# Keys and queries turned per pair of heads, and the globals' scores moved to other PSUM banks

## The chip, the cores and the metric

The kernel runs on one core of a Trainium2 chip. The metric is the device time of one launch in microseconds (us), the median of several runs. Five engines work beside each other and meet through semaphores: TensorE (PE), VectorE (DVE), ScalarE (ACT), GpSimd (POOL) and SyncE (SP), which issues most of the DMA transfers.

## The reference

Three layers follow one another: an attention with local and global tokens, a soft mixture of experts, and a mixture of experts with one expert a token. Only the first is touched.

```python
# q_l, k_l, v_l: (4, 8, 512, 64); q_g, k_g, v_g: (4, 8, 32, 64); window = 32
k_all = np.concatenate([k_g, k_l], axis=2)
s_g   = scale * np.matmul(q_g, k_all.transpose(0, 1, 3, 2))   # globals see all 544 keys
out_g = np.matmul(sm(s_g), v_all)
mask  = np.abs(pos[:, None] - pos[None, :]) <= window
s_ll  = np.where(mask, scale * np.matmul(q_l, k_l.transpose(0, 1, 3, 2)), -1e9)
s_lg  = scale * np.matmul(q_l, k_g.transpose(0, 1, 3, 2))
out_l = np.matmul(sm(np.concatenate([s_lg, s_ll], axis=-1)), np.concatenate([v_g, v_l], axis=2))
x = concat(out_g, out_l) -> (2304, 512)
x = moe(x)    # phi (512, 32), 8 experts of 4 slots, w1 and w2
out = moe2(x) # top-1 of 8 experts, capacity 576
```

## The kernel before

**Units and steps.** The attention is cut into 8 units, each one batch and half of its heads (four heads, two pairs). A unit has four Local steps (128 queries of all four heads each) and one Global step (the 32 global queries of four heads). The Global stands after the second Local; in the first unit it stands last, and in the last unit first.

**What a step issues.** The steps are staggered. In step k the program issues A of step k (scores), B of step k−1 (transposes of the probabilities), D1 of step k−3 (transposes of the result x), C of step k−2 (probabilities times values) and D2 of step k−4 (router logits lp of x). Between them stand the transposes of the next unit's keys and queries, and in some steps work of the second layer. The order on PE and POOL is the order of this code; the order on DVE, ACT and SP is chosen by the framework's scheduler.

**Scores of a Local step.** A writes 16 small matmuls into one half of each of two PSUM banks, `sc0` and `sc1`; `turn()` alternates the halves. Four DVE instructions (L335) add the mask, take the row maximum and move the scores to SBUF as P, and four exponentials on ACT (L337) follow.

**Scores of a Global step.** Its 544 keys are written in four pieces (L397): 192 and 64 columns into the half of `sc0`, 192 into the half of `sc1`, and 96 into a tile of the pool ps_x (`sg`). Five DVE instructions (L400 to L404) make the row maximum, four ACT exponentials (L406) write P.

**Keys and queries.** Keys arrive in tiles of 2 x 96 tokens (three tiles and six transfers a unit; the last transfer has 32 tokens), since the key buffer `kext` holds blocks of 96 local keys followed by 32 global ones. A tile's four transposes (both pairs of heads) fill one PSUM tile pk, which DVE empties for one pair and ACT for the other (L297). Queries arrive in two tiles of 2 x 128 tokens; each tile's four transposes (pq) are emptied the same way into one of two buffers `qtr`.

**The other names.** pt and pts: transposed probabilities of a Local step and their SBUF copy; ptg, pgg and ptsg, pgsg: those of a Global step. px and pxg: products with the values. pxt, xt: transposed x and its copy. lp, lpg: logits in PSUM; lpt, lpsg: their SBUF copies. c1 and c2 hold values rearranged for queries that straddle blocks (c2's copy on ACT is L280). The PSUM pool ps_tr has four banks, which pk, pq, pt, pxt, lp, ptg, pgg and some tiles of the second layer share.

**Transfers.** A unit's values come in eight transfers (v_g, five of 96 tokens, two of 32). All of these are issued on SP, in one queue with the 32 weight transfers of 1 MB each.

Of the kernel before, what the change touches and what calls it, by code (L numbers as in the profile page):

```python
# [37 lines left out]
def kernel(  # L38
# [119 lines left out]
    with ExitStack() as actx:  # L158
# [6 lines left out]
        qpool = actx.enter_context(tc.tile_pool(name="qpool", bufs=2))  # L165
# [20 lines left out]
        qtr = [persm.tile([128, 2, 256], F32, name=f"qtr{i}") for i in range(NQ)]  # L186
# [50 lines left out]
        def load_k(b, hf, g):  # L237

            hs = slice(4 * hf, 4 * hf + 4)
            knt[b, hf, g] = t = kpool.tile([96, 2, 4, 64], F32, tag="kn", name=f"kn{b}{hf}{g}")  # L240
            for m in range(2):
                n = 32 if m and g == 2 else 96
                o = 192 * g + 96 * m
                nc.sync.dma_start(t[0:n, m], k_l[b, hs, o:o + n].rearrange("h p d -> p h d"))

        def load_q(b, hf, j):
            hs = slice(4 * hf, 4 * hf + 4)
            t = qpool.tile([128, 2, 4, 64], F32, tag="qn", name=f"qn{b}{hf}{j}")
            for i in range(2):
                o = 256 * j + 128 * i  # L250
                nc.sync.dma_start(t[:, i], q_l[b, hs, o:o + 128].rearrange("h p d -> p h d"))
            qnt[b, hf, j] = t
# [35 lines left out]
        def unit_T(b, hf, g):  # L288
            ke, kn = kext[(2 * b + hf) % NB2], knt[b, hf, g]
            ps = ps_tr.tile([128, 2, 2, 96], F32, tag="tr", name=f"pk{b}{hf}{g}")  # L290
            for m in range(2):
                n = 32 if m and g == 2 else 96
                for pr in range(2):
                    T.transpose(ps[:, pr, m, 0:n], kn[0:n, m, 2 * pr:2 * pr + 2].rearrange("p h d -> p (h d)"), ident[0:n, 0:n])
            if g < 2:
                for pr, copy in enumerate((V.tensor_copy, S.copy)):
                    copy(ke[:, pr, 256 * g:256 * g + 256].rearrange("d (m c) -> d m c", m=2)[:, :, 0:96], ps[:, pr])  # L297
            else:
                V.tensor_copy(ke[:, :, 512:608], ps[:, :, 0])
                S.copy(ke[:, :, 640:672], ps[:, :, 1, 0:32])  # L300

        nqb = [0]
        qbs = {}

        def pair_Q(b, hf, j):
            qbs[b, hf, j] = qt = qtr[nqb[0] % NQ]
            nqb[0] += 1
            qn = qnt[b, hf, j]
            ps = ps_tr.tile([128, 2, 2, 128], F32, tag="tr", name=f"pq{b}{hf}{j}")
            for pr in range(2):  # L310
                for t in range(2):
                    T.transpose(ps[:, pr, t], qn[:, t, 2 * pr:2 * pr + 2].rearrange("p h d -> p (h d)"), ident)
            for pr, copy in enumerate((V.tensor_copy, S.copy)):
                copy(qt[:, pr].rearrange("d (t q) -> d t q", t=2), ps[:, pr])

        class Local:
# [5 lines left out]
            def A(self):  # L322
                ke, qt, u = kext[self.i], qbs[self.b, self.hf, self.u // 2], self.u
# [3 lines left out]
                for pr in range(2):  # L327
                    for c in range(4):
                        blk = 4 * u + c
                        o = 0 if blk == 0 else 544 if blk == 15 else 32 * (blk - 1 + (blk - 1) // 3)  # L330
                        for hp in range(2):
                            x = slice(64 * hp, 64 * hp + 64)
                            T.matmul(ps[hp][32 * c:32 * c + 32, pr], lhsT=qt[x, pr, 32 * (blk % 8):32 * (blk % 8) + 32], rhs=ke[x, pr, o:o + 128], start=True, stop=True, skip_group_check=True)  # L333
# [38 lines left out]
            def D2(self):  # L372
# [7 lines left out]
                V.tensor_copy(lpt[r, 128 * u:128 * u + 128], lp[r])  # L380

        class Global:
# [5 lines left out]
            def A(self):  # L388
                b, hf, ke = self.b, self.hf, kext[self.i]
                p1, p2 = turn()  # L390
                p3 = ps_x.tile([128, 96], F32, tag="x", name=f"sg{self.n}")

                lo = ke[:, :, 0:640].rearrange("p a (m c) -> p a m c", c=128)[:, :, :, 0:96]
                for ps, kk in ((p1[:, 0:192].rearrange("p (m c) -> p m c", c=96), lo[:, :, 0:2]), (p1[:, 192:256], ke[:, :, 608:672]),
                               (p2[:, 0:192].rearrange("p (m c) -> p m c", c=96), lo[:, :, 2:4]), (p3, lo[:, :, 4])):
# [3 lines left out]
                mx = work.tile([128, 5], F32, tag="mxg", name=f"mxg{self.n}")  # L399
                V.tensor_reduce(mx[:, 0:1], p1, AX.X, ALU.max)  # L400
                V.tensor_reduce(mx[:, 1:2], p2[:, 0:192], AX.X, ALU.max)
                V.tensor_reduce(mx[:, 2:3], p3, AX.X, ALU.max)
                V.tensor_reduce(mx[:, 3:4], mx[:, 0:3], AX.X, ALU.max)
                V.tensor_scalar_mul(mx[:, 4:5], mx[:, 3:4], -0.125)  # L404
                for o, ps in ((0, p1[:, 0:192]), (192, p2[:, 0:192]), (384, p3), (480, p1[:, 192:256])):
                    S.activation(P[:, o:o + ps.shape[1]], ps, AF.Exp, bias=mx[:, 4:5], scale=0.125)  # L406

            def B(self):
# [4 lines left out]
                V.tensor_copy(self.pts[0:96], pt)  # L413
# [201 lines left out]

        LQ = 2
        load_k(*units[0], 0)
        load_g(gnat_k, k_g, (0,))
        load_q(*units[0], 0)
        load_k(*units[0], 1)  # L620
        load_k(*units[0], 2)
        load_v(*units[0])
        spread_g(*units[0])
        load_q(*units[0], 1)
# [5 lines left out]
        unit_T(*units[0], 0)  # L630
# [3 lines left out]
        pair_Q(*units[0], 0)  # L634
        unit_T(*units[0], 1)
        unit_T(*units[0], 2)
# [5 lines left out]
        for k in range(ns - 1):  # L642
# [3 lines left out]
            j = (nloc + 1) // 2  # L646
            if u >= 0 and nloc % 2 and 2 * j < nl:
                pair_Q(*units[j // 2], j % 2)
# [5 lines left out]
            knext = []  # L654
            for g in range(3) if k == T0 else (u - (n < len(units) - 2),) if n and (u >= 0 and n == len(units) - 2 and u < 3 or u > 0 and n < len(units) - 2) else ():
                if n + 1 < len(units):
                    unit_T(*units[n + 1], g)
                    if g < 2:
                        unit_G(*units[n + 1], g)
                    if n + 2 < len(units):  # L660
                        knext.append(g)
# [17 lines left out]
            for g in knext:  # L679
                load_k(*units[n + 2], g)  # L680
# [19 lines left out]
            if k < ns:  # L700
                if u >= 0:
                    j = nloc // 2 + LQ
                    if nloc % 2 == 0 and 2 * j < nl:
                        load_q(*units[j // 2], j % 2)
                    if nloc == 0:
                        for g in range(3):
                            load_k(*units[1], g)
# [746 lines left out]
```

## Time and profile before

| | |
|---|---|
| median of 3 runs | 312.44 us (309.96 to 313.95) |
| profiled execution | 313.62 us, of which the span from the first to the last instruction is 311.8 us |
| mean granted TensorE clock | 0.948 |
| attention | from the start to about 175 us |
| weight stage of the second layer (ph, L883) | from 175.6 us |
| third layer | to the end |

Busy time of an engine is given in us of the span. A wait of an engine is the idle time before an instruction, with the instruction that ended it. The clock is given as a share of full speed.

### The profile page before, as it was taken

The page shows a single profiled execution, that of the slowest core. Times are in us where ns is not written, and L with a number is a line of the kernel's source. Part 1 is how long each engine was busy: PE and PEld are TensorE (multiplying, and loading weights), DVE is VectorE, ACT ScalarE, POOL GpSimd, SP SyncE. Part 2 cuts the span into 40 slices and gives each one's busy share as a digit, 9 for nine tenths or more (in the row PEclk, how much of TensorE's full clock was granted, in tenths as well). Part 3 has the DMA queues.
Part 4 walks back from the last instruction along what each step waited for, and adds up shares of the span by engine and source line. Part 5 has one row for each costly group of instructions (what it writes and reads, how often), then busy time and mean ns, then how long its engine had stood idle before and what let it go on. Part 6 is the DMA issues. An engine that isn't in the chain of part 4 may idle for free. (4 is left out here: it accounts for less than half of the span.)

```text
span 311.8 us, 10396 instructions
## 1 busy us (share of the span) xinstructions
PE 269.3 (86%) x4139; PEld 186.2 (60%) x4139; DVE 176.8 (57%) x763; ACT 136.7 (44%) x374; POOL 98.9 (32%) x191
## 2 busy tenths in 40 slices
PE   7778789879898988778689999998988699999992
PEld 5456567657676656566555644435456368877881
DVE  6364558657786866767775640016996479533100
ACT  2664537665667657754563110000452384132200
POOL 5815604640736454163223110011821001111121
PEclk9997879997999999999999999997899589999998
DMA  5766767787676897979689599999999200001010
GB/s 129 162 147 139 220 183 189 164 218 221 194 227 152 251 291 204 275 193 369 208 295 343 153 395 393 395 292 263 384 298 401 90 0 19 29 27 44 36 68 35
DMA packets 82896, 63.12 MB, mean 202 GB/s; under 512 B 57724, under 2 KB 65916, under 8 KB 82832
## 3 DMA queue, kind: packets, MB, share of 16 engines
q1 hardware_dynamic: 82144, 60.13, 63.9%
q0 software_dynamic: 688, 2.18, 1.9%
q8 instruction: 35, 0.57, 0.8%
q14 instruction: 29, 0.24, 0.2%
HBM read 55.66 MB, written 6.68 MB: 200 GB/s over the span
## 5 line engine op out<-in xcount | busy, mean ns | idle before, releaser
L337 ACT ACTIVATE P<-P,nmx 128x128 f32<-128x128 f32 x128 | 41.2, 391 | 21.5 <-DVE nmx L335 21.3
L335 DVE CUSTOM_DVE_ANT_0 P<-sc,mask 128x128 f32<-128x128 f32 x128 | 29.6, 285 | 14.7 <-PE sc L333 14.3
L333 PE MATMUL sc<-kext,qtr 64*32 64x128 f32 x1024 | 23.8, 289 | 11.4 <-ACT P L406 8.8
L271 POOL COPY c<-nat 32x520 f32<-32x520 f32 (+1 forms) x16 | 11.5, 721 | 68.0 <-PE px L355 47.0
L1222 POOL DMA_INDIRECT out_dram<-ys,idu x9 | 9.0, 998 | 71.1 <-ACT ys L1219 57.5
L346 ACT COPY pts<-pt 128x512 f32<-128x512 f32 (+1 forms) x32 | 18.1, 564 | 21.4 <-PE pt L345 21.4
L355 PE MATMUL px<-c,pts 128*32 128x65 f32 x640 | 23.1, 231 | 3.5 <-issue 3.5
L333 PEld LDWEIGHTS sc<-kext,qtr 64*32 64x32 f32 x1024 | 13.7, 110 | 19.6 <-ACT P L406 10.8
L355 PE MATMUL px<-nat,pts 128*32 128x65 f32 x384 | 22.8, 233 | 0.4 <-issue 0.4
L345 PE MATMUL pt<-ident,P 128*128 128x128 f32 x128 | 21.7, 295 | 0.0
L1183 ACT ACTIVATE hh<-phh 128x512 fp32r<-128x512 f32 x20 | 11.6, 598 | 21.2 <-PE phh L1180 15.1
L355 PEld LDWEIGHTS px<-c,pts 128*32 128x32 f32 x640 | 17.3, 114 | 6.0 <-issue 5.6
L1087 PE MATMUL pga<-oh,rec 128*128 128x128 f32 (+3 forms) x68 | 17.3, 349 | 3.8 <-DVE oh L1076 3.0
L1207 PE MATMUL py<-wh,hh 128*128 128x512 f32 (+1 forms) x72 | 20.3, 404 | 0.0
L1207 PE MATMUL py<-wl,hh 128*128 128x512 f32 (+1 forms) x72 | 20.0, 394 | 0.0
L1207 PE MATMUL py<-wh,hl 128*128 128x512 f32 (+1 forms) x72 | 19.4, 391 | 0.0
L355 PEld LDWEIGHTS px<-nat,pts 128*32 128x32 f32 x384 | 16.9, 115 | 2.6 <-issue 1.7
L1087 PEld LDWEIGHTS pga<-oh,rec 128*128 128x128 f32 x68 | 11.6, 208 | 10.2 <-DVE oh L1076 4.8
L345 PEld LDWEIGHTS pt<-ident,P 128*128 128x128 f32 x128 | 15.3, 149 | 2.8 <-issue 1.8
L1186 DVE SCALAR_TENSOR_TENSOR hl<-phh,hh 128x512 fp32r<-128x512 f32 x20 | 13.3, 688 | 5.6 <-ACT hh L1183 5.5
L883 PE MATMUL ph<-w,sT 128*32 128x256 f32 x256 | 15.9, 382 | 0.0
L1207 PEld LDWEIGHTS py<-wh,hh 128*128 128x128 f32 (+1 forms) x72 | 12.9, 186 | 4.3 <-ACT hh L1183 0.8
(307 smaller groups left out, 604.1 us busy)
## 6 DMA issues: line engine op xcount, KB each, us to landing
w<-in_moe_w_dram SPq DMA_DIRECT2D x32, 1024.0 KB, 7.4
out_dram<-zt SPq DMA_DIRECT2D x8, 544.0 KB, 10.2
qn<-in_q_l_dram SPq DMA_DIRECT2D x32, 128.0 KB, 5.4
w1b<-in_moe_w_dram SPq DMA_DIRECT2D x4, 1024.0 KB, 6.6
w2b<-in_moe_w_dram SPq DMA_DIRECT2D x8, 512.0 KB, 7.8
kn<-in_k_l_dram SPq DMA_DIRECT2D x40, 96.0 KB, 2.6
nat<-in_v_l_dram SPq DMA_DIRECT2D x40, 96.0 KB, 3.4
nat<-in_v_l_dram SPq DMA_DIRECT2D x16, 32.0 KB, 2.2
```

The costliest lines, as they stand in the source:

```text
L271: G.tensor_copy(c1[0:32, m0:m1], n[32:64, m0:m1])
L333: T.matmul(ps[hp][32 * c:32 * c + 32, pr], lhsT=qt[x, pr, 32 * (blk % 8):32 * (blk % 8) + 32], rhs=ke[x, pr, o:o + 128], start=True, stop= ...
L335: V.tensor_tensor_reduce(out=P[:, h], in0=ps[h % 2][:, h // 2], in1=mask[:, u], scale=-0.125, scalar=3.0e38, op0=ALU.add, op1=ALU.min, acc ...
L337: S.activation(P[:, h], P[:, h], AF.Exp, bias=nmx[:, h:h + 1], scale=-1.0)
L345: T.transpose(pt[:, c - h.start], self.P[:, c], ident)
L346: (V.tensor_copy if j else S.copy)(self.pts[:, h], pt)
L355: T.matmul(px[32 * c:32 * c + 32, h], lhsT=self.pts[:, h, 32 * c:32 * c + 32], rhs=vv[:, h], start=True, stop=True, skip_group_check=True)
L883: T.matmul(ph[32 * qf:32 * qf + 32], lhsT=sT[c // 2][:, c % 2], rhs=wt[:, c % 2, 256 * qf:256 * qf + 256], start=(c == 0), stop=(c == 3), ...
L1087: T.matmul(pga[0][:, 0:m], lhsT=rec[:, t], rhs=oh[0][:, q, 0:m], start=(k == 0), stop=(k == len(todo) - 1), skip_group_check=True)
L1183: S.activation(hh, ph[0], AF.Relu)
L1186: V.scalar_tensor_tensor(hl, ph[0], 0.0, hh.bitcast(F32), ALU.max, ALU.subtract)
L1207: T.matmul(py[0], lhsT=a[:, fc, o:o + nm], rhs=w[:, fc], start=(py[1] == 0), stop=(py[1] == 23))
```

## The change

Keys and queries of a unit are each loaded by four transfers of 128 tokens into one tile with four token blocks (both kinds share a pool of three buffers). Transposes go pair by pair: the four token blocks of one pair of heads fill one PSUM bank, and one engine empties it, DVE for the first pair and ACT for the second. For keys that is one copy of 480 and one of 32 columns, for queries one of 512. `qtr` holds a whole unit. Keys of the next unit are turned in the second and third Local step, queries of both pairs in the fourth.

Values come in seven transfers: v_g, one for each head (all 480 tokens of five blocks), and two of 32 tokens.

The Global's scores go into two tiles of ps_tr: `sg` with 480 columns and `sh` with 64. Four DVE instructions make the row maximum, two exponentials follow. The copy of lp to lpt (L380 before, L373 after) and the copy of ptg to ptsg (L413, L404) go from DVE to ACT.

```diff
-        qtr = [persm.tile([128, 2, 256], F32, name=f"qtr{i}") for i in range(NQ)]
+        qtr = [persm.tile([128, 2, 512], F32, name=f"qtr{i}") for i in range(NQ)]
...
+        def load_kq(to, name, src, b, hf, ts):
+            hs = slice(4 * hf, 4 * hf + 4)
+            if ts.start == 0:
+                to[b, hf] = kpool.tile([128, 4, 4, 64], F32, tag="kq", name=f"{name}{b}{hf}")
+            for t in range(ts.start, ts.stop):
+                nc.sync.dma_start(to[b, hf][:, t], src[b, hs, 128 * t:128 * t + 128].rearrange("h p d -> p h d"))
...
-            for m in range(6):
-                w = 96 if m < 5 else 32
-                nc.sync.dma_start(n[0:w, m, :, 0:64], v_l[b, hs, 96 * m:96 * m + w].rearrange("h p d -> p h d"))
+            for h in range(4):
+                nc.sync.dma_start(n[0:96, 0:5, h, 0:64], v_l[b, 4 * hf + h, 0:480].rearrange("(m p) d -> p m d", p=96))
+            nc.sync.dma_start(n[0:32, 5, :, 0:64], v_l[b, hs, 480:512].rearrange("h p d -> p h d"))
...
+        def turned(x, pr, ts, name):
+            ps = ps_tr.tile([128, ts.stop - ts.start, 128], F32, tag="tr", name=f"{name}{pr}{ts.start}")
+            for t in range(ts.start, ts.stop):
+                T.transpose(ps[:, t - ts.start], x[:, t, 2 * pr:2 * pr + 2].rearrange("p h d -> p (h d)"), ident)
+            return ps.rearrange("d t p -> d (t p)")
...
+        def unit_Q(b, hf, pr, copy, ts=slice(0, 4)):
+            copy(qtr[(2 * b + hf) % NQ][:, pr, 128 * ts.start:128 * ts.stop], turned(qnt[b, hf], pr, ts, f"pq{b}{hf}"))
...
-                V.tensor_copy(lpt[r, 128 * u:128 * u + 128], lp[r])
+                S.copy(lpt[r, 128 * u:128 * u + 128], lp[r])
...
-                p1, p2 = turn()
-                p3 = ps_x.tile([128, 96], F32, tag="x", name=f"sg{self.n}")
+                p1 = ps_tr.tile([128, 480], F32, tag="tr", name=f"sg{self.n}")
+                p2 = ps_tr.tile([128, 64], F32, tag="tr", name=f"sh{self.n}")
...
-                for o, ps in ((0, p1[:, 0:192]), (192, p2[:, 0:192]), (384, p3), (480, p1[:, 192:256])):
-                    S.activation(P[:, o:o + ps.shape[1]], ps, AF.Exp, bias=mx[:, 4:5], scale=0.125)
+                for o, ps in ((0, p1), (480, p2)):
+                    S.activation(P[:, o:o + ps.shape[1]], ps, AF.Exp, bias=mx[:, 3:4], scale=0.125)
...
-                V.tensor_copy(self.pts[0:96], pt)
+                S.copy(self.pts[0:96], pt)
...
+            if nx and u == 3:
+                unit_Q(*nx, 0, V.tensor_copy)
...
+            for pr in range(2) if k == T0 else (u - 1,) if n and 0 < u < 3 else ():
+                if nx:
+                    unit_T(*nx, pr, S.copy if pr else V.tensor_copy)
+                    unit_G(*nx, pr)
+            if nx and u == 3:
+                unit_Q(*nx, 1, S.copy)
```

**First place: PE in the Global step of the fifth unit.** Before, from the previous Global's logits (lpg) through the four score pieces (L397) to pxt; the numbers behind the names are those of single buffers, and a matmul of this type is two instructions where the row has x2:

```order
L452 MATMUL lpg_2021<-xtg_1898,phi_sb 32x32 x2
L397 MATMUL sc_172<-kext_161,qgbd 64x192 x2
L397 MATMUL sc_172<-kext_161,qgbd 64x64 x2
L397 MATMUL sc_173<-kext_161,qgbd 64x192 x2
L397 MATMUL sg_2029<-kext_161,qgbd 64x96 x2
L345 MATMUL pt_2050<-ident,P_1931 128x128 x4
L368 MATMUL pxt_2056<-ident,x_2004 128x128 x2
```

After:

```order
L443 MATMUL lpg_1930<-xtg_1816,phi_sb 32x32 x2
L389 MATMUL sg_1938<-kext_158,qgbd 64x480 x2
L389 MATMUL sh_1939<-kext_158,qgbd 64x64 x2
L338 MATMUL pt_1953<-ident,P_1851 128x128 x4
L361 MATMUL pxt_1959<-ident,x_1917 128x128 x2
```

The score pieces are two instead of four, and none of them names a bank `sc`, which the next Local step's scores use; the order around them is the same.

**Second place: ACT in the same step and the start of the next.** Before:

```order
L280 COPY c_166<-nat_162 64x520
L346 COPY pts_2049<-pt_2050 128x512
L370 COPY xt_2059<-pxt_2056 128x256
L406 ACTIVATE P_2038<-sc_172,mxg_2039 128x192
L406 ACTIVATE P_2038<-sc_173,mxg_2039 128x192
L406 ACTIVATE P_2038<-sg_2029,mxg_2039 128x96
L406 ACTIVATE P_2038<-sc_172,mxg_2039 128x64
L337 ACTIVATE P_2087<-P_2087,nmx_2088 128x128 x4
L370 COPY xt_2136<-pxt_2133 128x256
```

After:

```order
L276 COPY c_163<-nat_159 64x520 x2
L339 COPY pts_1952<-pt_1953 128x512
L363 COPY xt_1962<-pxt_1959 128x256
L397 ACTIVATE P_1944<-sg_1938,mxg_1945 128x480
L397 ACTIVATE P_1944<-sh_1939,mxg_1945 128x64
L373 COPY lpt<-lp_1986 64x128
L330 ACTIVATE P_1990<-P_1990,nmx_1991 128x128 x4
L404 COPY ptsg_2021<-ptg_2016 96x512
L302 COPY kext_160<-pk_2028 128x5x96
```

Four exponentials have become two, and the copies of lpt and ptsg stand in ACT's row, ptsg behind the four exponentials of the next Local step.

**Third place: ACT in the fourth Local step of the unit.** Before, from a key copy (kext) through the exponentials (P) and the query copy (qtr) to xt:

```order
L297 COPY kext_163<-pk_2125 128x2x96
L337 ACTIVATE P_2175<-P_2175,nmx_2176 128x128 x4
L314 COPY qtr_167<-pq_2201 128x256
L346 COPY pts_2208<-pt_2209 128x512
L300 COPY kext_163<-pk_2215 128x2x32
L370 COPY xt_2225<-pxt_2222 128x256
```

After:

```order
L363 COPY xt_2039<-pxt_2036 128x256
L373 COPY lpt<-lp_2068 64x128
L330 ACTIVATE P_2072<-P_2072,nmx_2073 128x128 x4
L339 COPY pts_2104<-pt_2105 128x512
L307 COPY qtr_165<-pq_2111 128x512
L363 COPY xt_2120<-pxt_2117 128x256
L373 COPY lpt<-lp_2173 64x128
```

The query copy has 512 columns instead of 256 and stands behind pts instead of ahead of it, and an lpt copy stands ahead of the exponentials.

## Rows read from the trace of the kernel before

**Rows 1.** The page: busy time of each engine in us, its share of the span, and the number of instructions.

```profile
PE 269.3 (86%) x4139; PEld 186.2 (60%) x4139; DVE 176.8 (57%) x763; ACT 136.7 (44%) x374; POOL 98.9 (32%) x191
```

**Rows 2.** Four of PE's waits from 25 to 160 us: engine, tile and line that waited, what ended the wait; us in total, times, longest us.

```profile
PE sc L333 <- ACT P L406: 8.8, 7, 1.8
PE pxg L427 <- issue: 4.1, 2, 2.2
PE px L355 <- issue: 2.6, 2, 2.2
PE lpg L452 <- ACT pts L346: 0.8, 3, 0.3
```

**Rows 3.** Stretches of time: length, then busy us and number of instructions of PE, PEld (PE's weight loads), DVE, ACT and POOL, then granted clock, DMA share and GB/s.

```profile
25.00:160.00 135.00, 113.19 (x2821) 84.10 (x2812) 93.37 (x495) 82.20 (x249) 60.34 (x89) 0.96 0.78 224
20.00:40.00 20.00, 15.18 (x294) 11.46 (x296) 10.65 (x49) 9.85 (x29) 9.77 (x14) 0.83 0.72 171
40.00:60.00 20.00, 18.06 (x440) 13.62 (x438) 13.97 (x76) 12.49 (x37) 6.36 (x10) 0.91 0.70 188
60.00:80.00 20.00, 16.64 (x380) 12.25 (x381) 13.81 (x72) 11.35 (x36) 8.07 (x13) 0.91 0.74 195
80.00:100.00 20.00, 16.96 (x468) 12.89 (x467) 14.01 (x76) 13.84 (x41) 11.23 (x18) 1.00 0.75 201
...
160.00:180.00 20.00, 18.44 (x302) 11.38 (x298) 12.85 (x54) 6.94 (x24) 3.78 (x25) 1.00 0.69 242
180.00:200.00 20.00, 19.54 (x248) 8.54 (x251) 3.59 (x15) 2.65 (x7) 1.86 (x9) 1.00 1.03 399
```

**Rows 4.** Timeline of PE from 95 to 102 us, a Global step of the fifth unit and the Local step behind it: start us, duration us, line and operation; in brackets the idle time before it and what ended that.

```profile
95.15 0.99 PE L397 MATMUL sc<-kext,qgbd 128*64 128x192 f32 x12
95.97 0.34 PE L397 MATMUL sg<-kext,qgbd 128*64 128x96 f32 x4
96.23 0.66 PE L345 MATMUL pt<-ident,P 128*128 128x128 f32 x4
96.72 0.38 PE L368 MATMUL pxt<-ident,x 128*128 128x128 f32 x2
...
97.54 0.39 PE L378 MATMUL lp<-xt,phi_sb 128*32 128x128 f32 x4
99.08 0.67 PE L333 MATMUL sc<-kext,qtr 64*32 64x128 f32 x32 [1.16 <-ACT P L406]
99.68 0.64 PE L411 MATMUL ptg<-ident,P 128*96 128x128 f32 x4
...
100.38 0.49 PE L294 MATMUL pk<-ident,kn 96*128 96x96 f32 x4
100.71 0.38 PE L368 MATMUL pxt<-ident,x 128*128 128x128 f32 x2
...
101.53 0.41 PE L378 MATMUL lp<-xt,phi_sb 128*32 128x128 f32 x4
101.88 0.34 PE L333 MATMUL sc<-kext,qtr 64*32 64x128 f32 x8
```

**Rows 5.** Timeline of ACT in the same place.

```profile
96.98 0.59 ACT L346 COPY pts<-pt 128x512 f32<-128x512 f32 x1 [0.66 <-PE pt L345]
...
97.86 0.73 ACT L406 ACTIVATE P<-sc,mxg 128x192 f32<-128x192 f32 x2
98.48 0.34 ACT L406 ACTIVATE P<-sg,mxg 128x96 f32<-128x96 f32 x1
98.70 0.32 ACT L406 ACTIVATE P<-sc,mxg 128x64 f32<-128x64 f32 x1
100.28 1.28 ACT L337 ACTIVATE P<-P,nmx 128x128 f32<-128x128 f32 x4 [1.26 <-DVE nmx L335]
```

**Rows 6.** Timeline of DVE in the same place.

```profile
96.04 0.42 DVE L400 TENSOR_REDUCE mxg<-sc 128x1 f32<-128x256 f32 x1
...
96.64 0.25 DVE L402 TENSOR_REDUCE mxg<-sg 128x1 f32<-128x96 f32 x1
96.92 0.16 DVE L403 TENSOR_REDUCE mxg<-mxg 128x1 f32<-128x3 f32 x1
97.11 0.15 DVE L404 TENSOR_SCALAR mxg<-mxg 128x1 f32<-128x1 f32 x1
...
97.97 0.29 DVE L380 COPY lpt<-lp 64x128 f32<-64x128 f32 x1
...
100.80 0.68 DVE L413 COPY ptsg<-ptg 96x512 f32<-96x512 f32 x1
```

**Rows 7.** Three of ACT's waits from 25 to 160 us, in the columns of rows 2.

```profile
ACT P L337 <- DVE nmx L335: 19.7, 22, 1.4
ACT c L280 <- PE lpg L452: 1.3, 1, 1.3
ACT c L280 <- POOL nat L265: 1.3, 1, 1.3
```

**Rows 8.** The start: one wait of PE in the first 25 us, and one row of SP's timeline (start, time for the issues together, number of transfers).

```profile
PE pqg L229 <- DMA xgt<-in_q_g_dram: 1.8, 1, 1.8
17.39 1.93 SPq L203 DMA_DIRECT2D xgt<-in_q_g_dram  x4
```

**Rows 9.** Waits from 160 us to the end, the longest of PE and three of SP's queue.

```profile
PE pga L1087 <- DVE oh L1076: 3.0, 1, 3.0
SPq L152 <- DVE parts L521: 6.5, 1, 6.5
SPq L152 <- PE sc L333: 4.9, 1, 4.9
SPq L148 <- PE px L355: 3.5, 1, 3.5
```

**Rows 10.** All matmuls of line L883, the weight stage: durations in ns (least, median, most), first and last start in us.

```profile
L883 PE MATMUL ph<-w,sT x256: 379/379/403, 175.6 to 202.7; 128*32 128x256 f32 x128
```

More of the change, by code (lines that the diff above doesn't have):

```diff
@@ L235, with load_k, load_q @@
         qnt, knt = {}, {}
-        def load_k(b, hf, g):
+        def load_kq(to, name, src, b, hf, ts):
             hs = slice(4 * hf, 4 * hf + 4)
[L240 to L252, printed above, removed]
+            if ts.start == 0:
+                to[b, hf] = kpool.tile([128, 4, 4, 64], F32, tag="kq", name=f"{name}{b}{hf}")
+            for t in range(ts.start, ts.stop):
+                nc.sync.dma_start(to[b, hf][:, t], src[b, hs, 128 * t:128 * t + 128].rearrange("h p d -> p h d"))
+        def load_k(b, hf, ts=slice(0, 4)):
+            load_kq(knt, "kn", k_l, b, hf, ts)
+        def load_q(b, hf, ts=slice(0, 4)):
+            load_kq(qnt, "qn", q_l, b, hf, ts)
         def load_v(b, hf):
@@ L286, in unit_G @@
                  kgt[:, 2 * hf + pr, None, 32 * b:32 * b + 32].to_broadcast([128, 5, 32]))
[L288 to L314, printed above, removed]
+        def turned(x, pr, ts, name):
[3 more added lines that the diff above has]
+            return ps.rearrange("d t p -> d (t p)")
@@ new lines, in unit_T @@
+        def unit_T(b, hf, pr, copy, ts=slice(0, 4)):
+            ke = kext[(2 * b + hf) % NB2][:, pr]
+            ps = turned(knt[b, hf], pr, ts, f"pk{b}{hf}")
+            k0, k1 = 4 * ts.start, 4 * ts.stop
+            a, z = -(-k0 // 3), k1 // 3
+            pieces = [(3 * a, 3 * z)] + [(x, y) for x, y in ((k0, 3 * a), (3 * z, k1)) if x < y]
+            for x, y in pieces:
+                o = 32 * (x + x // 3)
+                i = ps[:, 32 * (x - k0):32 * (y - k0)]
+                if y - x >= 3:
+                    copy(ke[:, o:o + 128 * (y - x) // 3].rearrange("d (m c) -> d m c", c=128)[:, :, 0:96], i.rearrange("d (m c) -> d m c", c=96))
+                else:
+                    copy(ke[:, o:o + 32 * (y - x)], i)
@@ L629 @@
         tw(TW[5])
-        unit_T(*units[0], 0)
+        unit_T(*units[0], 0, V.tensor_copy, lo)
+        unit_T(*units[0], 1, S.copy, lo)
         globals_k(True)
@@ L633 @@
         unit_G(*units[0], 1, S.copy)
-        pair_Q(*units[0], 0)
-        unit_T(*units[0], 1)
-        unit_T(*units[0], 2)
+        unit_Q(*units[0], 0, V.tensor_copy, lo)
+        unit_Q(*units[0], 1, S.copy, lo)
+        unit_T(*units[0], 0, V.tensor_copy, hi)
+        unit_T(*units[0], 1, S.copy, hi)
         V.tensor_tensor(i4, ident[:, 0:32], ident[:, 32:64], ALU.add)
@@ L645 @@
             st.A()
-            j = (nloc + 1) // 2
-            if u >= 0 and nloc % 2 and 2 * j < nl:
-                pair_Q(*units[j // 2], j % 2)
+            nx = units[n + 1] if n + 1 < len(units) else None
+            n2 = units[n + 2] if n + 2 < len(units) else None
+            if nx and u == 3:
+                unit_Q(*nx, 0, V.tensor_copy)
+            if nloc == 1:
+                for pr, copy in enumerate((V.tensor_copy, S.copy)):
+                    unit_Q(*units[0], pr, copy, hi)
             if 0 <= k - 1 < ns:
@@ L653 @@
                 globals_q()
[L654 to L661, printed above, removed]
+            for pr in range(2) if k == T0 else (u - 1,) if n and 0 < u < 3 else ():
[4 more added lines that the diff above has]
+                unit_Q(*nx, 1, S.copy)
             if 0 <= k - 3 < ns:
@@ L678 @@
                 mix(*units[n + 1], 0)
-            for g in knext:
-                load_k(*units[n + 2], g)
+            if n2 and u == 0:
+                if n:
+                    load_k(*n2)
+                else:
+                    load_q(*nx)
+            if n2 and u == 3:
+                if not n:
+                    load_k(*n2)
+                load_q(*n2)
             if k in events and events[k][0] is E1:
```

34 lines of the change are left out of this document (13 added, 21 removed).

## The prediction

> **What bounds the kernel now.** I read the engine table first [rows 1]: TensorE (PE) is busy 86% of the span, VectorE (DVE) 57%, ScalarE (ACT) 44%. Then the stretch in which all of the change lies, 25 to 160 us [first line of rows 3]: PE works 113.2 of 135 us, DVE 93.4, ACT 82.2, and the DMA engines have a share of 0.78. The waits of PE there name no DMA at all; [rows 2] has four of them. The largest single one is `sc L333 <- ACT P L406`, 8.8 us in 7 waits: a Local step that follows a Global may not write its scores until ScalarE has read the Global's scores out of the same two banks. The rest of PE's idle time is small and scattered, or is called issue (6.7 us in its two largest lines), which no part of the change addresses. So in this stretch PE's own stream sets the pace, and a wait on PE is worth its full length until some other chain is next.
>
> One such place in detail [rows 4 to 6]: the Global's scores start at 95.15, the last work of its step (lp) at 97.54, and the Local's sc only at 99.08, after 1.16 us idle. Where nothing is waited for, sc starts 0.35 us after lp (101.53 and 101.88 in the same rows), so without the wait it would start near 97.9. What holds it is the chain of five DVE instructions (96.04 to 97.26) and four exponentials on ACT (97.86 to 99.02).
>
> After 160 us PE waits for other engines, not for a DMA (the longest wait is 3.0 us, [rows 9]), and the queue that loads the weights itself waits for instructions of the attention (`PE sc`, `DVE parts`, `PE px`). So I let an earlier end of the attention move the end of the kernel by the same amount.
>
> **The change part by part.**
>
> *Globals' scores in their own banks.* The seven waits go: −8.8 us. In their place stands the wait of ptg, which is next on PE after sc. One exponential of 480 elements replaces four. Two of 192 take 0.62 us from start to start, one of 96 takes 0.22 [rows 5]: 0.94 ns an element, so 480 cost about 0.58, with a tail of 0.13 (the last one's 0.32 less 0.19 by that slope) about 0.71. Started at 97.86, as now, it ends at 98.57; ptg would be wanted at 97.9 + 0.60 (sc's start to ptg's start, rows 4) = 98.5. That is 0.1 us a Global, 0.7 in all. In the second unit the new order puts the lpt copy ahead of the exponentials, which then wait for lp: 0.3 more. I take +1.0; the bounds are 0 and 0.4 us in each of the seven, 2.8. DVE's part hardly moves the start: five instructions (1.22 us) become four; a reduction of 480 from the slope of 256 and 96 elements (0.42 and 0.25, so 1.06 ns an element) is 0.66, and with 0.21 for 64 elements, 0.16 and 0.15 the sum is 1.18.
>
> PE's score pieces go from four to two per pair of heads, with the same 544 columns. Now they take 1.08 us (95.15 to 96.23), of which the last 96 columns take 0.26 and the first 448 take 0.82, so a fixed share is visible. Between 0 and 0.45 us is saved a Global; I take 0.15, the end nearest to equal columns: −1.2 us for eight.
>
> *Keys and queries turned per pair of heads.* Twelve transposes of a unit's keys become eight, but the columns stay 512 per pair. Four of 96 take 0.33 us (100.38 to 100.71), four of 128 take 0.49 (96.23 to 96.72) [rows 4]: two full tiles of 96 and a last one of some 0.27 make 0.93, two tiles of 128 make 0.98. I book 0; the bounds are −0.2 and +0.1 a unit. The queries have as many transposes as before, both tiles now in the last Local step.
>
> The copy of the second query half is one of 512 elements on ACT, behind exponentials and pts [the orders of the third place]. The next unit's first sc needs it. ACT has, from the step's first ready exponential on, 1.28 us of exponentials and two 512-element copies of 0.59 [rows 5], 2.5 us; PE has sc, the transposes of q in two tiles, pt and pxt, the Global's px and lp, some 3.5 us by the same rows, but the exponentials start about 1 us into the step (sc at 99.08, first exponential at 100.28). The two ends fall together: 0 to 0.3 a unit, +0.15 in six units, +0.9 us.
>
> *lpt and ptsg copies on ACT.* DVE gives back 0.29 us four times and 0.68 once a unit [rows 6], and ACT takes about as much. PE does not run on either engine's sum here, but the banks do: sg and sh hold two of the four banks of ps_tr during a Global's step, and pxt of a step now waits for an lpt copy that stands in ACT's queue behind whatever is there. The nearest row is `lpg <- ACT pts`, 0.3 us at most [rows 2]. From 0 to 0.3 a unit in seven units; +1.0 us.
>
> *Transfers.* Keys and queries are loaded whole units ahead and PE waited for none of them after 25 us, so 18 issues a unit becoming 15 are worth nothing there. All four value transfers of a unit now wait for the last px of the unit before the last, but values are used about a unit after that. At the start it counts: the globals' queries (xgt) hold PE for 1.8 us, and 34 transfers up to the last of them become 31, at about 0.5 us an issue [rows 8]: −1.5; later first values may give some back. I take −1.2, bounds −1.8 and +1.
>
> *Sum.* −8.8 + 1.0 − 1.2 + 0 + 0.9 + 1.0 − 1.2 = −8.3 us. The profiled execution took 313.62 us, so 305.3; it stood 1.2 us over the median of the runs, which gives 304.1 us. With every bound at its low end the sum is −15.4 (297.0), at its high end about 0 (312.5). Bounds will not all fall together; the forecast's own range is 300 to 308.
>
> **The rivals.**
>
> *Larger pieces come later.* ptg could once start on the first exponentials while the last ran, and a query half came as 256 elements; now each is a single piece. If DVE hands over 0.3 us later than I count, the wait of ptg is 0.4 in seven places (2.8), the boundary wait 0.3 in six (1.8), and the banks cost 0.3 in seven (2.1): −8.8 + 2.8 + 1.8 + 2.1 − 1.2 − 1.2 = −4.5, or 307.9. For it: the 0.1 us that I find at 98.5 is the difference of two estimates. Against it: ACT is 61% busy, and its longest-lasting wait in this stretch, 19.7 us in 22 places, is for DVE's row maxima [rows 7], which follow PE's scores at once, so ACT moves earlier with PE. The Trainium skill, "Perfetto Trace Analysis", section "Optimizing Scalar/DVE Operations", speaks for this rival: where ScalarE and VectorE aren't saturated but leave bubbles on other engines, it would break instructions up so that work completes sooner, and the change does the reverse. No row of before shows a 480-element piece.
>
> *The clock gives more.* From 20 to 80 us the granted clock was 0.83 to 0.91, from 80 to 200 us 1.00, the upper of its two levels (2.4 GHz) throughout [rows 3]. If an unbroken stream keeps the upper level from 40 us on, 34.7 us of PE work at 0.91 shrinks by 3.1: 301.0. Against it: the breaks there are mostly issue waits [rows 2], which stay.
>
> *The gain is lost behind the attention.* DMA engines are full from 180 us on [last line of rows 3]. If the weights cannot start earlier although the attention ends earlier, half of 8.3 is lost: 308.2. Against it: PE waits for no DMA there, and 160 to 180 us shows a share of 0.69, that is, a stream that was held back by the attention's instructions [rows 9].
>
> *Slower: ACT's queue stops at a c copy and holds a bank.* Two c copies (L280) a unit stand in ACT's order, and ACT has stopped there for 1.3 us once on PE and once on GpSimd [rows 7]. Before, lpt and ptsg were emptied by DVE meanwhile; now they stand in the same queue, and PE's next transposes wait for their banks. At 14 such copies it decides from 0.6 us each (8.3 us); at the 1.3 of the rows it costs 18.2 and gives 322.3. Against it: two such stops were seen in 135 us, and the order shows the lpt copy a step away from them.
>
> **How the numbers follow.** I give the forecast 0.52, the larger pieces 0.25, the clock 0.10, the weights 0.06, the slower case 0.07. About 2% is what a measurement of this kernel can tell from no change: 306.2 to 318.7. Faster is nearly all of the forecast (0.50) and the clock: 0.60. Same is the rest of the forecast, the larger pieces and the weights: 0.33. Slower: 0.07. The range reaches from under the clock case to the high end of the bounds, 298 to 311.5, and leaves out the slower case and the tails.
>
> **What the profile of the changed kernel would show.** PE's wait of sc for the Global's exponentials is absent, and ptg waits under 0.2 us for the 480-element one; if it waits 0.4 or more, the larger pieces are right. The first sc of a unit waits for the qtr copy by 0 to 0.3 us. The weight stage, whose first matmul started at 175.6 us [rows 10], starts near 167. DVE's busy time in the attention falls by about 2 us a unit and ACT's rises by about 1. The prediction is wrong if waits on lpt, pts or ptsg copies add up to more than 3 us on PE, if ACT's lines show idle time at the c copies with PE behind it, or if the attention ends 8 us earlier and the end does not.

## The result and the profile after

The changed kernel takes 298.65 us (295.88 to 301.42) where the kernel before took 311.89 beside it: ratio 0.9545, interval 0.944 to 0.965. Every ratio here leaves out, on both sides, the runs that took over 1.5% longer than the fastest of their kernel, so it is not the quotient of the medians. In a later comparison the same kernel gave 0.963 (0.956 to 0.970). The forecast was 304.1 us, a ratio of 0.973. The direction was right; the size was not, and the time, taken as the ratio times the time before (297.7 to 298.2), lies at the low edge of the range of 298 to 311.5 us or under it.

The page's line for the engines, after:

```profile
PE 264.1 (90%) x4043; PEld 181.8 (62%) x4043; DVE 168.6 (57%) x707; ACT 143.4 (49%) x382; POOL 98.5 (33%) x191
```

Against [rows 1] PE's busy time has fallen by 5.2 us, DVE's by 8.2, and ACT's has risen by 6.7. The prediction had about 2 us a unit for DVE, twice what came, and about 1 for ACT, in eight units.

The weight stage, the answer to [rows 10]:

```profile
L879 PE MATMUL ph<-w,sT x256: 378/379/404, 161.3 to 188.4; 128*32 128x256 f32 x128
```

The attention ends 14.3 us earlier than in the first profile of before (175.6), and the rest, from there to the end of the span, takes 132.8 us instead of 136.2. The prediction had 8 and 0. Part of the 14.3 is chance: in the first profile of before the clock fell for long stretches [rows 3], and a second one (below) ended its attention at 172.4.

Waits of PE from 20 to 155 us, the answer to [rows 2]; columns as there:

```profile
PE px L348 <- issue: 3.9, 2, 2.7
PE sc L326 <- issue: 3.5, 3, 2.4
PE px L348 <- POOL kext L281: 2.4, 1, 2.4
PE pxg L418 <- issue: 1.4, 1, 1.4
PE pxtg L433 <- ACT pts L339: 0.7, 1, 0.7
PE ptg L402 <- ACT P L397: 0.5, 2, 0.3
PE pqg L228 <- DMA xgt<-in_q_g_dram: 0.4, 1, 0.4
```

The wait of sc behind the Global's exponentials is gone, all 8.8 us of it, and ptg waits 0.5 us in two places, 0.3 at the longest. Timeline of PE and then of ACT at a Global step after, the answer to [rows 4, 5]:

```profile
86.28 0.31 PE L389 MATMUL sh<-kext,qgbd 128*64 128x64 f32 x4
86.53 0.66 PE L338 MATMUL pt<-ident,P 128*128 128x128 f32 x4
...
87.92 0.41 PE L371 MATMUL lp<-xt,phi_sb 128*32 128x128 f32 x4
88.26 0.67 PE L326 MATMUL sc<-kext,qtr 64*32 64x128 f32 x32
89.13 0.64 PE L402 MATMUL ptg<-ident,P 128*96 128x128 f32 x4 [0.20 <-ACT P L397]
...
89.82 0.60 PE L288 MATMUL pk<-ident,kn 128*128 128x128 f32 x4
90.26 0.38 PE L361 MATMUL pxt<-ident,x 128*128 128x128 f32 x2
```

```profile
88.41 0.66 ACT L397 ACTIVATE P<-sg,mxg 128x480 f32<-128x480 f32 x1 [0.28 <-DVE rz L350]
88.97 0.31 ACT L397 ACTIVATE P<-sh,mxg 128x64 f32<-128x64 f32 x1
89.30 0.26 ACT L373 COPY lpt<-lp 64x128 f32<-64x128 f32 x1
89.59 1.28 ACT L330 ACTIVATE P<-P,nmx 128x128 f32<-128x128 f32 x4
90.89 0.58 ACT L404 COPY ptsg<-ptg 96x512 f32<-96x512 f32 x1
```

sc follows lp at once (0.34 us), and ptg waits 0.20 us for the exponential of 480 elements, which takes 0.56 us to the next start (0.58 was worked out). Stretches of time, the answer to [rows 3], with its columns (the granted clock is the last but two):

```profile
20.00:40.00 20.00, 19.37 (x454) 14.35 (x457) 15.56 (x74) 15.56 (x46) 8.69 (x13) 1.00 0.86 189
40.00:60.00 20.00, 15.78 (x378) 11.53 (x374) 11.28 (x61) 13.60 (x38) 11.59 (x17) 0.95 0.89 233
60.00:80.00 20.00, 18.36 (x460) 13.30 (x460) 12.81 (x67) 14.13 (x42) 10.23 (x16) 0.96 0.91 236
```

### The profile page after: what moved, and what is told of

Same layout as the page of the kernel before. It is cut to its first block, busy times and chain, and to the rows that moved or that the text cites. A ratio compares the mean times of both kernels' runs of the same rounds, so it can differ in the third digit from the quotient of the medians.

```text
span 294.1 us, 10151 instructions
## 1 busy us (share of the span) xinstructions
PE 264.1 (90%) x4043; PEld 181.8 (62%) x4043; DVE 168.6 (57%) x707; ACT 143.4 (49%) x382; POOL 98.5 (33%) x191
## 5 line engine op out<-in xcount | busy, mean ns | idle before, releaser
L338 PE MATMUL pt<-ident,P 128*128 128x128 f32 x128 | 22.9, 302 | 0.0
L348 PEld LDWEIGHTS px<-nat,pts 128*32 128x32 f32 x384 | 16.3, 112 | 3.9 <-issue 3.5
L350 DVE TENSOR_SCALAR rz<-px 128x4 f32<-128x4 f32 x32 | 5.1, 159 | 18.3 <-PE px L348 14.8
```

The source lines that it names most:

```text
L338: T.transpose(pt[:, c - h.start], self.P[:, c], ident)
L348: T.matmul(px[32 * c:32 * c + 32, h], lhsT=self.pts[:, h, 32 * c:32 * c + 32], rhs=vv[:, h], start=True, stop=True, skip_group_check=True)
```

## The experiments

Each ratio is against runs of the kernel before on the same chip. In the tables "attention" is the start of the weight stage's first matmul in the profile, "rest" the time from there to the end of the span. The ratios are what the verdicts rest on; they come from 6 to 12 runs each, except that before_again is one run for a second profile. One profile's attention moves by some us with the clock.

### The parts of the change, alone and in pairs

Three parts: the Global's scores in new banks (B), transfers and transposes (T), lpt and ptsg copies on ACT (C).

| kernel | parts | ratio (interval) | attention | rest |
|---|---|---|---|---|
| before, two profiles | none | 1 | 175.6, 172.4 | 136.2, 136.9 |
| banks_only | B | 0.985 (0.978 to 0.992) | 168.0 | 135.9 |
| turn_only | T | 0.985 (0.979 to 0.991) | 165.2 | 136.2 |
| copies_act_only | C | 0.988 (0.983 to 0.993) | 166.2 | 135.3 |
| banks_copies | B, C | 0.971 (0.964 to 0.978) | 165.8 | 134.6 |
| rest_only | T, C | 0.975 (0.969 to 0.982) | 163.7 | 135.2 |
| copies_dve | B, T | 0.984 (0.977 to 0.991) | 165.4 | 136.8 |
| after_again | B, T, C | 0.963 (0.956 to 0.970) | 161.8 | 133.1 |

**banks_only** puts the changed Global.A into the kernel before:

```diff
-                p1, p2 = turn()
-                p3 = ps_x.tile([128, 96], F32, tag="x", name=f"sg{self.n}")
+                p1 = ps_tr.tile([128, 480], F32, tag="tr", name=f"sg{self.n}")
+                p2 = ps_tr.tile([128, 64], F32, tag="tr", name=f"sh{self.n}")
...
```

> The kernel before with one edit: the Global's scores in two tiles of ps_tr (480 and 64 columns), with two exponentials; keys, queries, values and copies as before. If the removed wait carries the result, as the sum had it: the 8.8 us of sc behind L406 go, 0.5 to 1 us comes back at ptg, 1.2 us is saved on the score pieces, so about -9 us, 302 to 304. If the relief of DVE by the two moved copies or the transposes carry it: -3 to -5 us, about 307. If the banks run short without the rest of the change: 310 or more.

The gain, 1.5% or 4.7 us, is that of the second case (3 to 5 us) and about half of what the sum had. Its waits of PE in the attention:

```profile
PE pq L312 <- DMA qn<-in_q_l_dram: 4.0, 2, 3.4
PE pqg L229 <- ACT pts L346: 1.9, 1, 1.9
PE pt L345 <- ACT qtr L314: 1.9, 1, 1.9
```

The new exponentials hold PE for 0.2 us (at ptg), but queries from a DMA (4.0 us), and ACT's pts and qtr copies (3.8 us) now end last: in the first profile of before, queries and q_g cost 2.7 together. So in this profile some 5 of the 8.8 us stand again as other waits. It is one profile, of a run 1.8 us over the median, and that these waits are what took the gain is not shown: banks_copies (below) has 5.5 us of waits for queries and comes out at 0.971.

**rest_only** is the reverse edit, in the changed kernel.

> The changed kernel with the Global's scores put back into the halves of sc0 and sc1 and the tile of ps_x (four pieces, four exponentials, five DVE instructions); transfers, transposes and moved copies stay. If the wait carries the result: the 8.8 us are back, and what is left is the key transposes (2.1 us less by the start-to-start times of the two traces) and the start (about 2 us): -4 us, 307 to 309. If the transposes and transfers carry it: 301 to 303.

0.975, or 7.6 us less, which is between the two cases: the rest alone is worth more than the banks alone. PE still waits 6.9 us for the Global's exponentials there.

**copies_dve** and **copies_act_only** move the two copies back, or alone (the diff is that of copies_dve; copies_act_only is its reverse in the kernel before):

```diff
-                S.copy(lpt[r, 128 * u:128 * u + 128], lp[r])
+                V.tensor_copy(lpt[r, 128 * u:128 * u + 128], lp[r])
...
-                S.copy(self.pts[0:96], pt)
+                V.tensor_copy(self.pts[0:96], pt)
```

> The changed kernel with the copies of lpt and ptsg put back on DVE. If moving them is worth nothing, since PE runs on neither engine's sum: 297 to 300, as the changed kernel. If DVE's relief is needed to let the earlier PE run: 301 or more. If ACT's queue holds banks: 295 to 296.

> The kernel before with only the copies of lpt and ptsg moved from DVE to ACT. The Local step still waits for the Global's exponentials, so PE gains nothing from DVE's relief unless DVE's 2 us a unit stood ahead of what PE waits for: by the prediction 1.00; if DVE's relief counts by itself, 0.985.

Moving the copies is worth 1.2% alone and about 2% in the changed kernel (0.984 against 0.963). The prediction had put 1.0 us of cost there.

**turn_only** is rest_only with the copies on DVE. **banks_copies** is banks_only with them on ACT. **after_again** is the changed kernel.

> The transfers and transposes of the change alone: the Global's scores in their old banks, the copies of lpt and ptsg on DVE. If the transposes and the start are what the sum left out (2.1 us by the start-to-start times of the two traces, and 2.3 us of waits for q_g and q at the start): -4.4 us, ratio 0.986. If the sum was right to book nothing for them beside the start: -1.2 us, 0.996. If they carry most of the result: 0.975 or less.

> The kernel before with the Global's scores in ps_tr and with the copies of lpt and ptsg on ACT, old transfers and transposes. If the two parts need each other (in the changed kernel PE reaches work that DVE has not finished): 0.970 or less, where the new banks alone gave 0.985. If the copies are worth nothing: 0.985 again.

> The changed kernel itself, beside the runs of the kernel before of this call, so that the parts below have a whole to be measured against. By the first result 4.5% faster, ratio 0.955; by the sum of the prediction 0.973.

All three parts are worth 1.2 to 1.5% alone; their sum is 4.2%, the whole 3.7%. They do not need each other much, except that banks and transposes together (0.984) give no more than one of them. The table has four pairs of kernels that differ by the banks alone: these are worth 1.5% (against before), 1.7% (copies_act_only), 1.2% (rest_only) and 0.1% (turn_only), so at most some 5 us of the 8.8 in any of them.

**before_again**, no edit:

> The kernel before once more, for a second profile. The first one took 313.6 us where the runs beside it lay around 308, and its granted clock was 0.83 from 20 to 50 and from 70 to 80 us. If that is what made it long, a run of 306 to 309 us has the same waits behind L406 (8 to 9 us) and its attention ends some 4 us earlier, near 171 us, with a higher clock before 80 us.

It took 311.1 us, over the 306 to 309 named. The waits behind L406 were 8.8 us again; the attention ended 3.2 us earlier, with a granted clock of 0.94 and 0.97 from 20 to 40 and 40 to 60 us where the first profile had 0.83 and 0.91.

### Keys alone, and the small transposes

**k_pairs_only** takes only the keys' transfers, transposes and copies (load_kq, turned, unit_T) into the kernel before.

> The kernel before with only the keys changed: four transfers of 128 tokens, four transposes of a pair into one bank, emptied by one engine. The start-to-start times of the two traces make that 1.16 us a unit before and 0.88 after: -2.1 us, ratio 0.993. By the prediction, which went by columns: 1.00. If keys are what carries the transfers and transposes as a whole (0.985): 0.985 to 0.988.

0.994 (0.990 to 0.998), about −1.7 us, as the start-to-start times have it. Timeline of PE at a unit's third key tile before, and at a tile of 128 tokens in k_pairs_only:

```profile
103.40 0.57 PE L294 MATMUL pk<-ident,kn 96*128 96x96 f32 x4
103.90 0.44 PE L368 MATMUL pxt<-ident,x 128*128 128x128 f32 x2
```

```profile
104.10 0.60 PE L294 MATMUL pk<-ident,kn 128*128 128x128 f32 x4
104.54 0.38 PE L378 MATMUL pxt<-ident,x 128*128 128x128 f32 x2
```

The third tile took 0.50 us to the next work, and not the 0.27 that the prediction worked out by columns; a tile of 128 took 0.44. **small_x3** does the two small transposes three times:

```diff
+                    for _ in range(3 if n == 32 else 1):
                         T.transpose(ps[:, pr, m, 0:n], kn[0:n, m, ...], ident[0:n, 0:n])
```

> The kernel before with the two transposes of 32 tokens in each unit's third key tile done three times over (32 more of them in all). The prediction put the third tile at 0.27 us, so 0.05 us for a transpose of 32 tokens: +1.6 us, about 313.5. The trace of before shows 0.50 us from the third tile to the next work where a full tile of 96 takes 0.33; if the small ones make up that difference each costs 0.17: +5.3 us, about 317.

```profile
103.85 0.82 PE L295 MATMUL pk<-ident,kn 96*128 96x96 f32 x8
104.60 0.44 PE L369 MATMUL pxt<-ident,x 128*128 128x128 f32 x2
```

Four more take 0.25 us (0.75 against 0.50), 0.06 each, near the prediction's 0.05. In time nothing can be told: the medians are 308.6 and 308.1 us, and the ratio, from three runs, is 0.989 (0.981 to 0.997), faster although work was added. One ratio within about 1% of 1 is therefore weak evidence here, whatever its interval, and that holds for the keys' 0.994 too. So it is not the small ones by themselves; the tile with two sizes takes 0.2 us that neither size explains, and I have no run for that.

### The start and the queries

**qg_early** loads q_g ahead of the second unit's keys; **banks_q_early** gives banks_only queries two steps earlier.

```diff
+                        load_g(gnat_q, q_g, range(B))
                         for g in range(3):
                             load_k(*units[1], g)
...
-                        load_g(gnat_q, q_g, range(B))
```

```diff
-        qpool = actx.enter_context(tc.tile_pool(name="qpool", bufs=2))
+        qpool = actx.enter_context(tc.tile_pool(name="qpool", bufs=3))
...
-        LQ = 2
+        LQ = 3
...
```

> The kernel before with the globals' queries (q_g) loaded ahead of the second unit's keys instead of behind them; nothing else. PE waited 1.8 us for them near 20 us, and the clock was 0.83 for the 30 us behind it. If only the wait counts: -1.5 us, ratio 0.995. If the clock behind it counts as well: -3 us or more, 0.990. If the keys of the second unit are then late: 1.00.

> The new banks alone, but with each half unit's queries loaded two Local steps earlier (three buffers instead of two). With the new banks alone PE waited 4.0 us for queries from a DMA, 3.4 us in one place, and the clock was 0.71 behind it. If late queries ate the rest of the banks' gain: ratio 0.972 to 0.976, where the banks alone gave 0.985. If they did not matter: 0.985.

Neither helps: 1.005 (0.998 to 1.012) and 0.990 (0.985 to 0.994; banks_only had 0.985). In qg_early the wait for q_g is gone, but queries then cost 2.8 us. In banks_q_early the wait for queries fell from 4.0 to 1.0 us, while q_g's is 2.0 and one for ACT's qtr copy 2.5. A wait at the start that is moved comes back at the next transfer or copy, so the start's −1.2 us of the prediction has no support by itself.

### What the copies on DVE have to do with the third layer

DVE's waits after the attention name a stall at keyi, in the third layer, that nothing else explains ("issue"). Before, after, and in copies_act_only:

```profile
DVE keyi L1371 <- issue: 4.6, 1, 4.6
```

```profile
DVE keyi L1367 <- issue: 0.2, 1, 0.2
```

```profile
DVE keyi L1371 <- issue: 0.2, 1, 0.2
```

In every kernel with the copies on DVE it is 3.4 to 4.6 us, in every one with the copies on ACT and no added writes 0.2 or less. It holds PE at pga (3.0 us, [rows 9]). The copies are 36 instructions; they are long over by then. **after_pad** and **copies_pad** put 36 one-element writes on DVE in front of the weight stage, **pad_early** puts them at the very start:

```diff
+        pad = mp.tile([1, 1], F32, name="pad")
+        for _ in range(36):
+            V.memset(pad, 0.0)
```

> The changed kernel with 36 one-element writes on DVE put in front of its work in the weight stage, where it is nearly idle. In every kernel with the lpt and ptsg copies on DVE (36 instructions in all), DVE stood still for 3.4 to 4.6 us at keyi in the third layer, named issue, and PE waited for it; with the copies on ACT this was 0.2 us. If that stall hangs on how many instructions DVE has had before, it is back: keyi 3 us or more, the time from the weight stage's first matmul to the end 135 to 137 us instead of 133, ratio about 0.972. If ACT doing the copies is what counts: 133 us and 0.963.

> The kernel before with only the copies moved to ACT, and the same 36 one-element writes on DVE. If the number of DVE instructions is what made that move worth 1.2%: ratio 0.997 to 1.00, with the keyi stall back. If DVE's relief in the attention counts: 0.988.

after_pad gave 1.003 (0.996 to 1.009) and copies_pad 1.007 (1.001 to 1.014): the keyi stall is back (4.6 and 3.3 us), but PE also waited 3.5 and 3.2 us for sT behind the writes themselves, so the two effects are mixed. The whole loss in after_pad, from 0.963 to 1.003, is larger than both together, and what else is in it is open.

> The changed kernel with the 36 one-element writes at the very start, in the 1.8 us in which DVE waits for GpSimd anyway, since in the weight stage they stood on PE's path (3.5 us at sT). If the stall at keyi hangs on the number of DVE instructions ahead of it: 3 us or more at keyi, 135 to 137 us from the weight stage's first matmul to the end, and the attention ends at 161 to 163 us; ratio 0.972 to 0.978. If it hangs on something else that the writes in the weight stage disturbed: keyi 0.2 us, 133 us, 0.963.

```profile
DVE keyi L1370 <- issue: 3.4, 1, 3.4
```

```profile
PE pga L1086 <- DVE oh L1075: 2.7, 1, 2.7
```

0.986 (0.978 to 0.994), and the rest takes 136.6 us instead of 133.1: the stall comes with the 36 instructions, whatever they do, and with it the rest is 3.5 us longer. (At the start the writes cost PE another 2.3 us, and one issue wait was longer, so the whole loss is more than that; 0.972 to 0.978 had been expected.)

The traces also hold the DMA packets that the page calls instruction, on queues of their own (packets, MB, share of 16 engines). On q14, in the 4.6 us up to keyi, before and after:

```profile
q14 instruction: 7, 0.06, 3.3%
```

```profile
q14 instruction: 1, 0.01, 0.4%
```

In all 13 profiles with the stall, 5 to 7 of these packets of 8 KB start within it; in the seven without it none does, and seven start in the 5 us behind keyi. So the stall goes with DVE's instructions being brought in; no run changes that transfer by itself.

### The values, and ACT's c copy

**v_old** puts the old value transfers into the changed kernel, **v_only** the new ones into the kernel before.

```diff
+            for m in range(6):
+                w = 96 if m < 5 else 32
+                nc.sync.dma_start(n[0:w, m, :, 0:64], v_l[b, hs, 96 * m:96 * m + w].rearrange("h p d -> p h d"))
...
```

> The changed kernel with the values loaded in the old way (five transfers of 96 tokens for all heads, one of 32). The prediction gave the new split nothing: 0.963. If what is left of the transfers' and transposes' share (0.985 together, keys alone 0.994) is in the values: 0.970.

> The kernel before with only the values loaded in the new way (one transfer a head). Taking that away from the changed kernel cost 2.5%. If the transfers by head are worth that much by themselves: 0.975 to 0.980. If only what is left of the transposes' and transfers' 1.5% beside the keys: 0.990. If they help only when PE is ahead, as in the changed kernel: 1.00.

v_old gives 0.989 (0.982 to 0.996), a larger loss than either case expected; v_only 0.993 (0.986 to 1.000), with medians of 307.4 us and 307.2 before. So the new transfers matter in the changed kernel and hardly alone. Waits of PE in v_old:

```profile
PE sc L326 <- issue: 5.9, 4, 2.6
PE px L348 <- issue: 4.9, 2, 2.9
PE pxg L418 <- issue: 3.9, 3, 1.5
PE px L348 <- ACT c L276: 2.0, 1, 2.0
```

Issue waits are 14.7 us there in these three lines (8.8 after). What they are, the instruction packets tell: in the 20 profiles PE has 91 issue waits of 0.8 us or more in the first 170 us, and each ends 1.2 to 1.7 us after a packet of 16 KB has landed on q8, though these packets come some 6 us apart. For the wait of 2.16 us before 69.12 us in the profile of before, the packet of the stretch from 66.5 to 68.2 us:

```profile
q8 instruction: 1, 0.02, 4.5%
```

So these waits go with PE's own instructions being brought in, though no run changes that by itself, and later there are a few, at pga, without such a packet. The prediction took the issue waits as a fixed share that the change leaves alone. Why these waits grow with the values' transfers no run here shows, and they are not all of it: with the new transfers all issue waits from 20 to 155 us are 8.8 us (after), 10.5 (after_again) and 11.7 (after_c2, below), against 15.0 in v_old, whose attention ends 7.4 us or more later than theirs.

**after_c2.** In the changed kernel ACT and PE at the Global of the seventh unit:

```profile
120.42 0.66 ACT L397 ACTIVATE P<-sg,mxg 128x480 f32<-128x480 f32 x1 [0.23 <-DVE mxg L395]
120.98 0.31 ACT L397 ACTIVATE P<-sh,mxg 128x64 f32<-128x64 f32 x1
121.31 1.15 ACT L276 COPY c<-nat 64x520 f32<-64x520 f32 x2
```

```profile
122.07 0.22 PE L348 MATMUL px<-c,pts 128*32 128x65 f32 x1 [2.38 <-POOL kext L281]
```

The two c copies run behind the exponentials, and px needs the first of them, which ends near 121.9; the releaser named, POOL's kext, ended at about the same moment, but px does not read it. This is the slower rival's mechanism, at one place instead of fourteen.

```diff
-            S.copy(c2[0:64, m0:m1], n[64:128, m0:m1])
+            (V.tensor_copy if (b, hf) == (3, 0) else S.copy)(c2[0:64, m0:m1], n[64:128, m0:m1])
```

> The changed kernel with the two c2 copies of the seventh unit on DVE instead of ACT. There ACT's order has them behind the Global's exponentials, PE waits 2.4 us at px, and the clock is 0.50 behind it. If ACT's queue holds them up, as the slower case of the prediction had it for one place: the 2.4 us are gone and 1 to 3 us of clock with them, ratio 0.952 to 0.957. If PE waits for the values themselves: 0.963 as before.

```profile
PE px L348 <- DVE c L276: 1.7, 1, 1.7
```

0.969 (0.962 to 0.975), no better than 0.963: on DVE the copies stand behind the Global's row maxima, and px still waits 1.7 us. No version tried beats the changed kernel.

## Why the prediction was right or wrong

**The bound and the removed wait: right.** PE's stream bounds the attention, the 8.8 us are gone, ptg waits 0.5 instead of 1.0 us. **Their worth: too high.** The sum took a removed wait at its full length and gave the new banks −9.0 us with the score pieces; banks_only gave 1.5%, 4.7 us, and no pair of kernels gave more than 1.7%. In the profile of banks_only some 5 us stand again as waits for queries and for ACT's copies.

**Score pieces: wrong.** From sg's start to pt's takes 1.07 us after in all eight places (117.51 to 118.58 at one), 1.08 before [rows 4]; the "fixed share" was not there, and nothing was saved.

**Keys: wrong by one term.** The step "a last one of some 0.27" measured 0.50, so a unit saves 0.28 us (1.16 against 0.88) and not 0; k_pairs_only gives −1.7 us, within the noise shown by small_x3. The row stood in the trace of before.

**The query copy at the unit's boundary: wrong.** +0.9 us was booked; no wait of that name appears after.

**lpt and ptsg on ACT: the step that failed most.** It read "PE does not run on either engine's sum here, but the banks do", and booked +1.0 us. The only wait of PE on a moved copy in the profile after is 0.3 us (sc behind lpt); pxtg (0.7) and lp (0.2) wait for pts, and before lpg waited 0.8 for it [rows 2]. So the cost was at most 0.3 us, and the move gained 1.2 to 2%, 3.7 to some 6 us, for which the sum had no term: the relief of DVE was booked at nothing. Of that, the third layer's stall at keyi is shown: the rest is 3.5 us longer with pad_early and 3.7 with copies_dve than in after_again, though only 0.9 to 1.6 in the three other pairs of the table with and without the copies. What copies_act_only gains beyond that is not explained.

**Transfers booked at nothing: wrong.** Taking back the values' part costs 2 to 2.5% of the changed kernel. The cause stays open.

**The sum as a whole: right in direction partly by luck.** By parts it had −9.0 us for the banks, −0.3 for transfers and transposes with the start, and +1.0 for the copies; alone they measured −4.7 (banks_only), −4.6 (turn_only) and −3.8 (copies_act_only). A term twice too large stood in for two that were missed.

**The end follows the attention: right**, and the rest shortened by itself, which no term had.

**The rivals.** Larger pieces did not come late (0.5 us at ptg), so the rule of the Trainium skill, "Perfetto Trace Analysis", section "Optimizing Scalar/DVE Operations", that would break them up had at most that half microsecond to win at ptg. The clock seemed to give more in the first profile pair: 0.83 and 0.91 before in the two stretches from 20 to 60 us, 1.00 and 0.95 after. In the second pair it is 0.94 and 0.97 before and 1.00 and 0.83 after, with a mean of 0.958 in both, so no gain of the clock is shown. The slower case is real at one place.

## What to carry to other kernels

A wait that PE loses is worth at most what the next chain leaves of it; look up, for the same place, which transfers and copies were ready with less room than the wait was long. Work moved off an engine also changes how many instructions that engine has had when it comes to a later, unrelated stage: compare "issue" stalls in the untouched stages before calling an effect local, and look for instruction packets beside them. And take start-to-start times of every form in a group, not the first one's by columns.

## What was not expected of the hardware

DVE's stall at keyi went from 0.2 to 3.4 us by 36 one-element writes some 200 us earlier, and it is there exactly in the profiles in which instruction packets arrive within it. PE's 91 issue waits of 0.8 to 3.8 us in the first 170 us of the 20 profiles all end 1.2 to 1.7 us after such a packet has landed.

The granted clock falls behind some gaps of PE and not behind others. Two gaps in the profile of before, and the stretches behind them in the columns of [rows 3], where the clock is the last but two:

```profile
61.12 0.67 PE L333 MATMUL sc<-kext,qtr 64*32 64x128 f32 x32 [1.15 <-ACT P L406]
...
69.12 0.24 PE L427 MATMUL pxg<-nat,ptsg 96*32 96x65 f32 x1 [2.16 <-issue]
```

```profile
60.00:62.00 2.00, 0.88 (x35) 0.68 (x36) 0.91 (x4) 1.07 (x4) 1.82 (x4) 1.00 0.55 123
62.00:64.00 2.00, 2.00 (x56) 1.63 (x62) 2.00 (x11) 1.65 (x6) 0.74 (x2) 1.00 0.82 175
...
68.00:70.00 2.00, 0.88 (x27) 0.69 (x29) 0.17 (x2) 0.00 (x0) 0.00 (x0) 1.00 0.65 105
70.00:72.00 2.00, 2.00 (x46) 1.27 (x40) 1.84 (x8) 0.00 (x0) 0.00 (x0) 0.72 0.76 263
72.00:74.00 2.00, 2.00 (x40) 1.46 (x40) 1.83 (x16) 1.69 (x6) 0.00 (x0) 0.50 1.07 342
```

Behind the 1.15 us wait for L406 it stays 1.00, 2.4 GHz; behind the 2.16 us at 69 us it goes to 0.50, 1.2 GHz, for some 3 us (worked out from the last two stretches). The length of a gap does not decide it alone: PE's issue wait of 2.19 us that ended at 133.28 us in the same profile was followed by no fall. Neither was any of the seven waits that the change removes (six of 1.15 to 1.2 us, one of 1.8), so in that profile they cost their length and no clock.
